# Swapping the two factors of a forward transform: 64 points first, then 47

## The chip, the cores and the metric

The kernel runs on one core of one Trainium2 chip. The metric is device time in microseconds (us) for one execution of the whole program; lower is better. Engines are named as in the profile: PE (matrix multiply) with PEld (its weight load), DVE, ACT, POOL and SP. DMAs are issued from the queues of SP, ACT and POOL.

## The reference

```python
def _attn_ref(x, w_r, w_i, b_r, b_i):          # x: (8, 3008, 256)
    X = np.fft.rfft(x, axis=1)
    Yr = X.real @ w_r - X.imag @ w_i + b_r
    Yi = X.real @ w_i + X.imag @ w_r + b_i
    Yr = np.sign(Yr) * np.maximum(np.abs(Yr) - 0.01, 0.0)
    Yi = np.sign(Yi) * np.maximum(np.abs(Yi) - 0.01, 0.0)
    return np.fft.irfft(Yr + 1j * Yi, n=3008, axis=1)

def _moe_ref(x, w_in, w_out):                   # x: (24064, 256), d_ff = 2048
    h = x @ w_in
    g = np.where(h > 0.0, h, np.exp(np.minimum(h, 0.0)) - 1.0)
    return g @ w_out
```

The output is the second function applied to the first one's result: a real Fourier transform along the sequence, a complex 256 x 256 product with a soft threshold, the transform back, and then a two-layer network with ELU over all 24064 rows.

## The kernel before

The sequence length is 3008 = 47 x 64, and each transform is done in two factor steps with matmuls against tables of sines. There are five kinds of unit work per batch, each a group of matmuls into one PSUM tile and one copy out of it:

- **A** (`unit_A`, matmul L126): the 47-point step. A chunk of x, `xts[ci]`, holds 94 rows in partitions 17 to 110 (the 17 others are zeroed in the first batch) and 8 sequence places of 256 columns. One unit is two matmuls of 512 columns; the copy (L109 or L107, 96 x 1024) goes to a tile A and from there to DRAM (DA). Eight units a batch, from four chunks.
- **X** (`unit_X`, L160): the 64-point step. `load_Z` reads DA back as Z, transposed between partitions and free dimension by that trip through DRAM: 128 partitions, 24 frequencies, 256 columns. One unit is 8 matmuls with Z as weights and 128 columns of the table M2; ACT copies 1024 columns to XT. Six units a batch, two for each group of 8 frequencies.
- **M** (`unit_M`, in the first batch `first_M`; L179): the complex product with `wcat_r` and `wcat_s`, four matmuls of 512 columns, bias on DVE (L186), soft threshold on POOL (L194, L195; in the first batch on POOL, ACT or DVE in turn). Twelve a batch. M needs the XT tile of its group of 8 frequencies.
- **B** (`unit_B`, L227): the 64-point step back with table M3; copy to Bz (L240), stored to DRAM (DB). Six a batch.
- **Y** (`unit_Y`, L267): the 47-point step back with table M4 from Bs, which `load_Bs` reads from DB: 8 matmuls of 96 rows and 94 columns and one copy of 752 columns, which gathers from PSUM with a stride. Eight a batch.

The second network works on blocks of 512 rows and pairs of 128 hidden columns: `front` (four matmuls of 512 columns, L594, then Exp on ACT), `elu`, and `back` (eight matmuls of 256 columns, L651), two slots behind. One batch is 6 blocks x 8 pairs = 48 slots. The transform units of the next batch (X, M, B), the A units of the batch after that and the Y units are fillers: `plan` puts at most one into each slot by a list written out by hand, and in a slot PE runs the filler, then `front`, then an earlier `back`. Every engine runs its own instructions in program order, and so does each queue.

```python
        mid = [
            ("X", 0), ("X", 1), ("M", 0, 0), ("M", 0, 1), ("X", 2), ("M", 1, 0), ("M", 1, 1),
            ...
            ("M", 5, 1), ("A", 0), ("B", 4), ("A", 1), ("B", 5), ("A", 2), ("A", 3), ("A", 4),
            ("A", 5), ("A", 6), ("A", 7),
        ]
```

Ahead of the slots stands the start. POOL makes index rows with iota and issues the loads of x (eight DMAs a batch, two for each chunk); DVE makes the phases and ACT the sines of M1 and M2 in three groups of 512 columns; between them the eight A units of batch 0 run with their copies and stores. Then Z is loaded, half from SP's queue and half from ACT's; M4 and M3 are made of M1 and M2 with transposes on PE. Once the second group of Z has landed (`gate`), POOL issues x of batch 1; SP issues `w_in`. X, M and B of batch 0 follow, the Bz tiles are stored (two buffers for three tiles), Bs is loaded, the eight A units of batch 1 run, w_in is scaled, and two Y units open the first slot. `idle_pe(n)` is n matmuls of 512 columns on constants, whose result is not used.

Of the kernel before, what the change touches and what calls it, by code (L numbers as in the profile page):

```python
# [12 lines left out]
F32R = mybir.dt.float32r  # L13

# [4 lines left out]
N1 = 47  # L19
# [3 lines left out]
P0 = N2 - N1  # L23
P1 = P0 + 2 * N1


@with_exitstack
def kernel(
# [23 lines left out]
    SIN_SCALE = 2.0 * math.pi / S * (1.0 - 3e-7)  # L52

    constp = ctx.enter_context(tc.tile_pool(name="constp", bufs=1))
    M1 = constp.tile([P1, 4 * K1], F32R, name="M1")
    M2 = constp.tile([P, 2, K1, N2], BF16, name="M2")
# [7 lines left out]
    lam_n = constp.tile([P, 1], F32, name="lam_n")  # L64

# [4 lines left out]
    wk4 = ctx.enter_context(tc.tile_pool(name="wk4", bufs=4))  # L70

# [23 lines left out]
    def load_x(b, ci):  # L95
        xv = x[b].rearrange("(r m c) d -> c r m d", c=4, m=8)
        for r0, r1 in ((0, 80), (80, 2 * N1)):
            nc.gpsimd.dma_start(xts[ci][P0 + r0 : P0 + r1], xv[ci, r0:r1].bitcast(F32R))

# [11 lines left out]
    def unit_A(b, u, alone=False, on_dve=False, ahead=False):  # L111
        ci, uu = u // 2, u % 2
        if uu == 0:
            if ahead and ci > 1:
                A_of[b, ci] = late3.tile([4 * K1, 8, D], BF16, name="A", tag="gT")
            elif alone:
                A_of[b, ci] = wk4.tile([4 * K1, 8, D], BF16, name="A", tag="Bs")
            else:
                A_of[b, ci] = wk2.tile([4 * K1, 8, D], BF16, name="A", tag="A")
            if ci == 0:  # L120
                DA_of[b] = dram.tile([NH, 4 * K1, D], BF16, name="DA", tag="DA")
        xt, A = xts[ci], A_of[b, ci]
        dav = DA_of[b].rearrange("(m c) r d -> c r m d", c=4)
        ps = unit_ps("aps", alone or ahead)
        for j in range(2):
            nc.tensor.matmul(  # L126
                ps[0 : 4 * K1, j, :], lhsT=M1[:],
                rhs=xt[:, 4 * uu + 2 * j : 4 * uu + 2 * j + 2, :], start=True, stop=True,
            )
        evac(  # L130
            A[:, 4 * uu : 4 * uu + 4, :].rearrange("p n d -> p (n d)"),
            ps[0 : 4 * K1].rearrange("p a b -> p (a b)"), on_dve,
        )
        if alone:
            nc.sync.dma_start(dav[ci, :, 4 * uu : 4 * uu + 4, :], A[:, 4 * uu : 4 * uu + 4, :])
        elif uu == 1:
            (nc.sync if ahead else nc.scalar).dma_start(dav[ci], A[:])

    def load_Z(b, k0, k1, n0, n1, engs):

        if b not in Z_of:
            Z_of[b] = zp.tile([P, K1, D], BF16, name="Z", tag="Z")
        for c in range(2):
            for h in range(2):
                r = h * 2 * K1 + c * K1
                q = c * N2 + h * NH
                engs[c].dma_start(
                    Z_of[b][q + n0 : q + n1, k0:k1, :], DA_of[b][n0:n1, r + k0 : r + k1, :]
                )

    def unit_X(b, u, alone=False, split=False):
        g, dt = u // 2, u % 2
        if dt == 0:
            XT_of[b, g] = wk3.tile([P, 2, 2, 8 * N2], BF16, name="XT", tag="XT")
        XT, Z = XT_of[b, g], Z_of[b]
        ps = unit_ps("xps", alone)
        psv = ps[:].rearrange("p a (k j) -> p (a k) j", j=P)
        for kk in range(8):
            k = 8 * g + kk
            nc.tensor.matmul(  # L160
                psv[:, kk, :], lhsT=Z[:, k, dt * P : dt * P + P], rhs=M2[:, :, k, :],
                start=True, stop=True,
            )
        xv = XT[:, dt].rearrange("p c (k j) -> p c k j", j=N2)
        pv = psv.rearrange("p k (c j) -> p c k j", c=2)
        if split:
            nc.scalar.copy(xv[:, :, 0:4], pv[:, :, 0:4])  # L167
            nc.vector.tensor_copy(xv[:, :, 4:8], pv[:, :, 4:8])
        else:
            nc.scalar.copy(xv, pv)  # L170
# [3 lines left out]
    def m_group(b, q, i, ps):  # L174
        XT = XT_of[b, q // 2]
        o = (2 * (q % 2) + i) * P
# [108 lines left out]
    idle_pe(20)  # L285
    xts = []
    for ci in range(4):
        xt = constp.tile([P1, 8, D], F32R, name=f"xt{ci}")
        xts.append(xt)
    with tc.tile_pool(name="stagep", bufs=1) as stagep:  # L290
# [4 lines left out]
        def iota(shape, name, pattern, base=0, cm=0):  # L295
            t = stagep.tile(shape, F32, name=name)
            nc.gpsimd.iota(
                t[:], pattern=pattern, base=base, channel_multiplier=cm,
# [4 lines left out]
        def col(name, src, s1, op0, s2=None, op1=None):  # L303
            t = stagep.tile([P, 1], F32, name=name)
            if op1 is None:
                nc.vector.tensor_scalar(t[:], src[:], s1, None, op0)
            else:
                nc.vector.tensor_scalar(t[:], src[:], s1, s2, op0, op1)
            return t

        def flat(t):
            return t.rearrange("p a b -> p (a b)")

        def zero_rows(ci):
            for m in range(0, 8, 2):
                nc.scalar.activation(
                    xts[ci][0:P0, m : m + 2, :].rearrange("p n d -> p (n d)"), busy[0:P0, :],
                    AF.Copy, scale=0.0,
                )

        pcol = iota([P, 1], "pcol", [[0, 1]], cm=1)
        k1row = iota([P1, 2, K1], "k1row", [[0, 2], [1, K1]])
        ph1 = iota([P1, 2, K1], "ph1", [[QUARTER, 2], [0, K1]], base=QUARTER)
        load_x(0, 0)
        kv = iota([P, K1, N2], "kv", [[1, K1], [N1, N2]])
        for ci in range(1, 4):
            load_x(0, ci)
        for ci in range(2, 4):
            nc.gpsimd.memset(xts[ci][0:P0].bitcast(F32), 0.0)
        ident = stagep.tile([P, P], F32, name="ident")  # L330
        nc.gpsimd.memset(ident[:], 0.0)
        nc.gpsimd.affine_select(
            out=ident[:], in_=ident[:], pattern=[[-1, P]], compare_op=ALU.not_equal,
            fill=1.0, base=0, channel_multiplier=1,
        )

        def wrap(v, r):
            nc.vector.tensor_scalar(r, v, 1.0 / S, CMAGIC, ALU.mult, ALU.add)
            nc.vector.tensor_scalar(r, r, -CMAGIC, -float(S), ALU.add, ALU.mult)
            nc.vector.tensor_tensor(v, r, v, ALU.add)  # L340


        half = col("half", pcol, 0.5, ALU.mult, -0.5 * P0 - 0.25, ALU.add)
        halfm = col("halfm", half, CMAGIC, ALU.add)
        n1col = col("n1col", halfm, -CMAGIC, ALU.add)
        n1s = col("n1s", n1col, float(N2), ALU.mult)
        v1 = stagep.tile([P1, 2 * K1], F32, name="v1")
        r1t = stagep.tile([P1, 2 * K1], F32, name="r1t")
        nc.vector.scalar_tensor_tensor(
            v1[:], flat(k1row[:]), n1s[0:P1, :], flat(ph1[:]), ALU.mult, ALU.add,  # L350
        )
        wrap(v1[:], r1t[:])
        zero_rows(0)
        nc.scalar.activation(r1t[:], v1[:], AF.Sin, bias=0.0, scale=SIN_SCALE)
        zero_rows(1)
        h1col = stagep.tile([P, 1], F32, name="h1col")
        nc.vector.scalar_tensor_tensor(
            h1col[:], n1col[:], -2.0, pcol[:], ALU.mult, ALU.add
        )
        h1col = col("h1m", h1col, float(-P0), ALU.add)  # L360
        isx = col("isx", pcol, P0 - 0.5, ALU.is_gt)
        h0col = stagep.tile([P, 1], F32, name="h0col")
        nc.vector.scalar_tensor_tensor(
            h0col[:], h1col[:], -1.0, isx[:], ALU.mult, ALU.add
        )
        nc.vector.tensor_tensor(h0col[:], h0col[:], isx[:], ALU.mult)
        nc.vector.tensor_tensor(h1col[:], h1col[:], isx[:], ALU.mult)
        ccol = col("ccol", pcol, N2 - 0.5, ALU.is_gt)
        n2col = stagep.tile([P, 1], F32, name="n2col")
        nc.vector.scalar_tensor_tensor(  # L370
            n2col[:], ccol[:], -float(N2), pcol[:], ALU.mult, ALU.add
        )
        ph2col = col("ph2col", ccol, -float(QUARTER), ALU.mult, float(QUARTER), ALU.add)
        M1f = stagep.tile([P1, 2, 2 * K1], F32, name="M1f")
        nc.vector.tensor_scalar(M1f[:, 0, :], r1t[:], h0col[0:P1, :], None, ALU.mult)
        nc.vector.tensor_scalar(M1f[:, 1, :], r1t[:], h1col[0:P1, :], None, ALU.mult)
        nc.vector.tensor_copy(M1[:], flat(M1f[:]))

        v2 = stagep.tile([P, K1, N2], F32, name="v2")
        u2 = stagep.tile([P, K1, N2], F32, name="u2")  # L380
        st = stagep.tile([P, K1, N2], F32, name="st")
        r2 = stagep.tile([P, 8, N2], F32, name="r2")

        def phases(g):

            gs = slice(8 * g, 8 * g + 8)
            nc.vector.tensor_scalar(
# [391 lines left out]
```

## Time and profile before

| what | value |
|---|---|
| three timed runs, median (lowest to highest) | 968.99 us (966.66 to 969.65) |
| the profiled execution's own time | 967.69 us |
| its span, first to last instruction | 965.8 us |
| granted PE clock, mean | 0.984 |
| PE / ACT / DVE / POOL busy | 96% / 74% / 76% / 30% |
| DMA traffic | 105.43 MB, 109 GB/s on the mean |

In the rows of a group a line reads: line, engine, operation, output <- inputs, shapes, count | busy time, mean ns of one | idle time of the engine before it and what ended that. In a window row each engine has its busy time and in brackets its count of instructions; then come the granted clock, the mean share of the 16 DMA engines (over 1 where packets overlap on one engine) and GB/s. In a timeline row and in the chain, the first number is the start in us from the first instruction and the second the duration.

### The profile page before, as it was taken

What the parts mean: (1) busy time and instruction counts of PE and PEld (TensorE: products, weight loads), DVE (VectorE), ACT (ScalarE), POOL (GpSimd) and SP (SyncE); (2) the same over time, 40 slices, a digit from 0 to 9 for tenths busy, and PEclk for the clock granted to TensorE, in tenths of its full rate; (3) what the DMA queues carried; (4) which work ended last, traced back from release to release, by engine and by line L of the source; (5) the groups of instructions that cost most, each with busy time, mean ns of one, the idle gap of its engine ahead of it and who ended that gap; (6) DMA issues with size and microseconds to landing.
All of it is one profiled execution on the core that took longest, in us unless ns stands there. A gap on an engine that the chain in (4) does not pass through costs nothing.

```text
span 965.8 us, 16747 instructions
## 1 busy us (share of the span) xinstructions
PE 927.7 (96%) x6482; PEld 654.1 (68%) x6482; DVE 737.0 (76%) x858; ACT 719.1 (74%) x816; POOL 286.5 (30%) x363
## 2 busy tenths in 40 slices
PE   7968999999999999999999999999999999999997
PEld 3425766777667766777667776677767776677775
DVE  8646677776778777886778767887778877888996
ACT  7436878688877778778786888877887788667654
POOL 5602531234302432125312343024421133321332
PEclk9959999999999999999999999999999999999999
DMA  9998824637176533827256461665338102411011
GB/s 215 239 239 182 129 77 125 165 59 129 45 191 122 87 77 82 223 52 118 67 142 159 67 125 50 181 133 87 77 82 212 32 22 67 109 45 41 23 44 42
DMA packets 113987, 105.43 MB, mean 109 GB/s; under 512 B 7794, under 2 KB 107636, under 8 KB 113012
## 3 DMA queue, kind: packets, MB, share of 16 engines
q1 hardware_dynamic: 45220, 56.19, 22.2%
q0 software_dynamic: 27680, 26.74, 19.4%
q10 hardware_dynamic: 41008, 21.43, 8.4%
q8 instruction: 51, 0.84, 0.4%
q14 instruction: 28, 0.23, 0.1%
HBM read 54.53 MB, written 49.81 MB: 108 GB/s over the span
## 4 chain that ended last, share of the span: by engine, by line
PE 59%; DVE 17%; ACT 13%; DMA 4%; issue 4%; ACTq 1%; POOL 1%; DVEq 0%; SPq 0%; POOLq 0%
PE ps_o L651 23%; PE hps L594 23%; PE mps L179 7%; DVE gT L614 6%; DVE gT L618 4%; ACT Et L604 3%; DVE Et L629 2%; PE aps L126 2%; ACT Et L601 2%; DVE Et L631 2%; ACT A L109 2%; DMA DA<-A 2%; ACT osb L663 2%; PE bps L227 1%; DMA DB<-Bz 1%
## 5 line engine op out<-in xcount | busy, mean ns | idle before, releaser
L651 PE MATMUL ps_o<-w_out_r,gT 128*128 128x256 f32 (+1 forms) x3072 | 490.5, 302 | 1.5 <-DVE gT L614 0.9
L651 PEld LDWEIGHTS ps_o<-w_out_r,gT 128*128 128x128 f32 (+1 forms) x3072 | 409.4, 187 | 66.3 <-DVE gT L614 13.0
L594 PE MATMUL hps<-yT,w_in_s 128*128 128x512 bf16 (+1 forms) x1536 | 389.0, 375 | 9.0 <-DVE gT L618 5.6
L604 ACT ACTIVATE Et<-hps 128x1024 f32<-128x1024 f32 (+1 forms) x300 | 302.2, 1007 | 104.1 <-PE hps L594 82.4
L614 DVE SCALAR_TENSOR_TENSOR gT<-Et,hps 128x1024 fp32r<-128x1024 f32 (+1 forms) x188 | 222.5, 1183 | 70.6 <-ACT Et L602 50.0
L618 DVE SCALAR_TENSOR_TENSOR gT<-hps,Et 128x1024 fp32r<-128x1024 f32 (+1 forms) x196 | 237.8, 1213 | 17.7 <-PE ps_o L651 1.5
L594 PEld LDWEIGHTS <-w_in_s 128*128 128x128 bf16 x1536 | 133.3, 98 | 150.2 <-issue 33.2
L631 DVE TENSOR_SCALAR Et<-Et 128x1024 f32<-128x1024 f32 (+1 forms) x196 | 134.6, 687 | 76.9 <-ACT Et L604 74.4
L629 POOL TENSOR_SCALAR Et<-Et 128x512 f32<-128x512 f32 (+1 forms) x104 | 64.7, 622 | 309.6 <-ACT Et L604 309.6
L194 POOL TENSOR_SCALAR clip<-yb 128x512 f32<-128x512 f32 x84 | 51.8, 616 | 293.4 <-DVE yb L186 231.2
L601 ACT ACTIVATE Et<-hps 128x1024 f32<-128x1024 f32 x84 | 86.5, 1029 | 68.6 <-PE hps L594 68.4
L195 POOL TENSOR_TENSOR Y<-yb,clip 128x512 bf16<-128x512 f32 x84 | 107.5, 1279 | 7.0
L186 DVE TENSOR_TENSOR yb<-mps,bias_bc 128x512 f32<-128x512 f32 x96 | 65.8, 689 | 34.6 <-PE mps L179 30.7
L602 ACT ACTIVATE Et<-Et 128x1024 f32<-128x1024 f32 x84 | 88.9, 1058 | 2.7
L109 ACT CAST A<-aps 96x1024 bf16<-96x1024 f32 x59 | 59.3, 1009 | 17.0 <-PE aps L126 11.0
L109 ACT CAST yT<-yps 128x752 bf16<-128x752 f32 x63 | 49.7, 790 | 14.9 <-PE yps L267 14.9
L179 PE MATMUL mps<-wcat_r,XT 128*128 128x512 bf16 x192 | 58.1, 383 | 0.3 <-ACT XT L167 0.2
L126 PE MATMUL aps<-xt,M 111*96 111x512 f32 x128 | 44.0, 436 | 14.1 <-ACT Bz L240 5.2
L629 DVE TENSOR_SCALAR Et<-Et 128x512 f32<-128x512 f32 (+1 forms) x104 | 56.8, 547 | 0.5 <-ACT Et L604 0.2
L179 PE MATMUL mps<-wcat_s,XT 128*128 128x512 bf16 x192 | 57.1, 379 | 0.0
L240 ACT CAST Bz<-bps 128x1024 bf16<-128x1024 f32 x47 | 47.4, 1008 | 9.7 <-DMA DB<-Bz 5.7
L170 ACT CAST XT<-xps 128x1024 bf16<-128x1024 f32 x46 | 46.0, 1001 | 7.9 <-PE xps L160 7.9
(96 smaller groups left out, 415.1 us busy)
## 6 DMA issues: line engine op xcount, KB each, us to landing
xt<-in_x_dram POOLq DMA_DIRECT2D x32, 640.0 KB, 6.1
out_dram<-osb SPq DMA_DIRECT2D x160, 128.0 KB
Bs<-DB SPq DMA_DIRECT2D x63, 192.0 KB
DB<-Bz ACTq DMA_DIRECT2D x21, 512.0 KB
DA<-A ACTq DMA_DIRECT2D x24, 384.0 KB
Z<-DA SPq DMA_DIRECT2D x28, 256.0 KB
Z<-DA SPq DMA_DIRECT2D x34, 128.0 KB
xt<-in_x_dram POOLq DMA_DIRECT2D x32, 112.0 KB, 5.8
```

What stands on the lines that cost most here:

```text
L109: nc.scalar.copy(dst, src)
L179: nc.tensor.matmul(ps, lhsT=XT[:, dt, c, o : o + P], rhs=wm[:, dt, :], start=(m == 0 and dt == 0), stop=(m == 1 and dt == 1),)
L195: nc.gpsimd.tensor_tensor(Y_of[b, q][:, i, :], yb[:], clip[:], ALU.subtract)
L594: nc.tensor.matmul(hps[:, s, 0:nb], lhsT=w_in_s[:, dt, ft * P : ft * P + P], rhs=yT[:, dt, bs : bs + nb], start=(dt == 0), stop=(dt == 1),)
L601: nc.scalar.activation(E_, hps[:, :, 0:nb], AF.Relu, scale=-1.0)
L602: nc.scalar.activation(E_, E_, AF.Exp, scale=-1.0)
L604: nc.scalar.activation(E_, hps[:, :, 0:nb], AF.Exp)
L614: nc.vector.scalar_tensor_tensor(gT[:, :, 0:nb], E_, -1.0, h_, ALU.add, ALU.max)
L618: nc.vector.scalar_tensor_tensor(gT[:, :, 0:nb], h_, 0.0, E_, ALU.max, ALU.add)
L629: eng.tensor_scalar(E_[:, s], E_[:, s], 1.0, 0.0, ALU.min, ALU.max)
L631: nc.vector.tensor_scalar(E_, E_, 1.0, -1.0, ALU.min, ALU.add)
L651: nc.tensor.matmul(po[q][0 : t1 - t0, i_ % 2, :], lhsT=gT[:, s, t0:t1], rhs=w_out_r[:, ft, :], start=(ft == 0 and i_ % 2 == 0), stop=(ft = ...
```

## The change

The two factors of the forward transform change places. The 64-point step comes first: x stands in 128 partitions (64 places at a 47 KB pitch in DRAM, and two halves of 24 places, which share one place), 8 places of 256 columns contiguous for each partition, so that three chunks hold a batch instead of four, and a load of a chunk is one DMA instead of two. A has six units with 128 output rows. The 47-point step follows in X: Z has 96 partitions and 32 frequencies, one unit has 8 matmuls of 96 columns, and there are eight units. The stores to DA are contiguous for 8 places (4 KB), and the loads of Z take pieces of 512 bytes. XT is one tile for the whole batch, and every M needs all eight X units; so `plan` and the start put all X ahead of all M. In the first batch the copies of X go to ACT and DVE in turn.

The tables: M1 and M2 get other phases, M2 in four groups of 384 columns from integer indices (an AND with 63 on DVE); M3 is no longer transposed from M2 but made of phases and four sines of 768 columns of its own, M4 on POOL. A first sine on a dummy loads ACT's table at the start, and the Exp table is loaded after B of batch 0. The `idle_pe` counts change: 20 to 9, 14 to 10, 10 to 6, and 2 after each of the first five A units instead of 4, 4 and 3.

The diff, cut to its core:

```diff
-    M2 = constp.tile([P, 2, K1, N2], BF16, name="M2")
+    M2 = constp.tile([2 * NR, NS, 2, 2 * K1], BF16, name="M2")      # 96 x 32 x 2 x 48
...
-    def load_x(b, ci):
-        xv = x[b].rearrange("(r m c) d -> c r m d", c=4, m=8)
-        for r0, r1 in ((0, 80), (80, 2 * N1)):
-            nc.gpsimd.dma_start(xts[ci][P0 + r0 : P0 + r1], xv[ci, r0:r1].bitcast(F32R))
+    def load_x(b, ci, m0=0, m1=8):
+        src = bass.AP(
+            tensor=x.tensor,
+            offset=x.offset + (b * S + 8 * ci + m0) * D,
+            ap=[[N1 * D, N2], [(NJ - 1) * D, 2], [D, m1 - m0], [1, D]],
+        )
+        nc.gpsimd.dma_start(xts[ci][:, m0:m1, :], src.bitcast(F32R))
...
-                ps[0 : 4 * K1, j, :], lhsT=M1[:],
+                ps[:, j, :], lhsT=M1[:],
...
     def load_Z(...):
-        for c in range(2):
-            for h in range(2):
-                r = h * 2 * K1 + c * K1
-                q = c * N2 + h * NH
-                engs[c].dma_start(
-                    Z_of[b][q + n0 : q + n1, k0:k1, :], DA_of[b][n0:n1, r + k0 : r + k1, :]
-                )
+        for c in range(2):
+            engs[c].dma_start(
+                Z_of[b][c * NR : c * NR + NR, s0:s1, :],
+                DA_of[b][c * NS + s0 : c * NS + s1].rearrange("s n d -> n s d"),
+            )
...
     def unit_X(...):
-                psv[:, kk, :], lhsT=Z[:, k, dt * P : dt * P + P], rhs=M2[:, :, k, :],
+                psv[:, kk, 0 : 4 * K1], lhsT=Z[:, k, dt * P : dt * P + P],
+                rhs=M2[:, k].rearrange("p c m -> p (c m)"), start=True, stop=True,
...
-            nc.scalar.copy(xv, pv)
+        xv = XT[:, dt].rearrange("p c (m s) -> p c m s", s=NS)[:, :, :, 8 * g : 8 * g + 8]
+        pv = psv[:, :, 0 : 4 * K1].rearrange("p k (c m) -> p c m k", c=2)
+        evac(xv, pv, on_dve)
...
+        def phases(g):                       # DVE, four groups
+            dve.tensor_scalar(m_, m_, 63, None, ALU.bitwise_and)
+            dve.scalar_tensor_tensor(k_, m_, float(N1), kk1[...], ALU.mult, ALU.add)
+            dve.tensor_scalar(v, kf, n1s[z], ph[z], ALU.mult, ALU.add)
+            dve.tensor_scalar(r, v, CMAGIC, -CMAGIC, ALU.add, ALU.add)
+            dve.tensor_tensor(v, v, r, ALU.subtract)
+            dve.tensor_scalar(st[z, gs], kf, S // 2 + 0.5, -0.5, ALU.is_gt, ALU.add)
+        def signs(g):                        # DVE; waits for sizes(g)
+            dve.scalar_tensor_tensor(a2[z, gs], a2[z, gs], qd[z], st[z, gs], ALU.subtract, ALU.mult)
+        def sizes(g):                        # ACT
+            nc.scalar.activation(a2[z, gs], v2[z, gs], AF.Abs)
...
+        sizes(3)
+        sines(2, 1)
+        signs(3)
+        slot0()
+        sines(3, 0)
+        sines(3, 1)
+        nc.scalar.activation(r4[:], v4[:], AF.Sin, bias=0.0, scale=TURN)
+        for g in range(4):
+            load_Z(0, 8 * g, 8 * g + 8, (nc.sync, nc.scalar))
...
+        nc.scalar.activation(a3[:], w3[:], AF.Abs)
+        dve.scalar_tensor_tensor(u3[:], a3[:], 0.25, st3b, ALU.subtract, ALU.mult)
...
+    for u in range(8):
+        unit_X(0, u, alone=True, on_dve=bool(u % 2))
+    for (c, o), src, sc, bi in (...):        # four sines of 128 x 768
+        nc.scalar.activation(M3[:, :, c, o * N2 : o * N2 + N2], src[:], AF.Sin, bias=bi, scale=sc)
     first_M(0, 0, nc.gpsimd)
-    fX(2)
     first_M(0, 1, nc.scalar)
...
-    for u in range(8):
+    for u in range(6):
         unit_A(1, u, on_dve=bool(u % 2), ahead=True)
...
-    idle_pe(10)
+    idle_pe(6)
...
+        mid = [("X", u) for u in range(8)] + [
+            ("M", 0, 0), ("M", 0, 1), ("M", 1, 0), ("M", 1, 1), ("B", 0), ("M", 2, 0),
+            ("M", 2, 1), ("B", 1), ("M", 3, 0), ("M", 3, 1), ("B", 2), ("M", 4, 0),
+            ("M", 4, 1), ("B", 3), ("M", 5, 0), ("M", 5, 1), ("A", 0), ("B", 4), ("A", 1),
+            ("B", 5), ("A", 2), ("A", 3), ("A", 4), ("A", 5),
+        ]
```

437 lines of the change are left out of this document (239 added, 198 removed), and 5 rows, old and new, of the table mid.

## The prediction

> **What bounds the kernel now.** I read the page first, then stages, then the chain, then single slots. The profiled execution took 967.69 us around a span of 965.8; the three timed runs have a median of 968.99, so a sum made on the profile is carried over by adding 1.3.
>
> ```profile
> PE 927.7 (96%) x6482; PEld 654.1 (68%) x6482; DVE 737.0 (76%) x858; ACT 719.1 (74%) x816; POOL 286.5 (30%) x363
> ...
> PEclk9959999999999999999999999999999999999999
> DMA  9998824637176533827256461665338102411011
> ```
>
> PE is full, except in the first three slices of 24 us, where the DMA engines are full instead and the granted clock once falls to a half. Before the first L594 matmul at 73.4 us nothing of the second network runs. From there the batches take 117.3 us, six times 113, and 99.6. The windows of that start and of one steady batch:
>
> ```profile
> 51.50:56.70 5.20, 0.03 (x1) 0.03 (x1) 0.00 (x0) 1.09 (x2) 0.00 (x0) 0.50 0.87 227
> 56.70:73.40 16.70, 13.50 (x42) 5.50 (x43) 7.86 (x9) 6.09 (x7) 2.25 (x3) 0.55 0.95 242
> ...
> 416.60:529.60 113.00, 112.29 (x806) 80.63 (x804) 86.82 (x97) 89.84 (x101) 32.80 (x40) 1.00 0.51 111
> ```
>
> The steady batch is 99% PE; the start has a 5.2 us hole and then a clock of 0.55. The chain of the first 80 us says what the start waits for:
>
> ```profile
> 21.84 1.28 ACT L447
> ...
> 25.99 5.02 DMA Z<-DA
> 31.82 5.22 POOL xt L98 x8
> ...
> 43.98 11.52 DMA DB<-Bz
> ...
> 57.86 2.27 DMA DB<-Bz
> ```
>
> To 20.5 us it is DVE making phases, then sines and a table load on ACT, which hold ACT's half of the Z loads; then eight x loads issued on POOL ahead of POOL's first soft threshold; then a store of Bz that takes 11.5 us, because x of batch 1 and w_in are on the DMA engines; then unit_A of batch 1. In the steady state the price of a filler unit is the distance of two L594 starts:
>
> ```profile
> 418.79 1.03 PE L594 MATMUL hps<-yT,w_in_s 128*128 128x512 bf16 x4
> ...
> 420.95 1.03 PE L594 MATMUL hps<-yT,w_in_s 128*128 128x512 bf16 x4
> ...
> 425.60 1.02 PE L594 MATMUL hps<-yT,w_in_s 128*128 128x512 bf16 x4
> ...
> 427.87 1.03 PE L594 MATMUL hps<-yT,w_in_s 128*128 128x512 bf16 x4
> ```
>
> A slot with a Y unit lasts 2.16, with an X unit 2.27; by the same reading A slots last 2.28 to 2.67, a bare slot 1.72 to 1.99.
>
> **The steady state.** Per batch 6 X + 8 A units become 8 X + 6 A: the same 32 fillers besides Y, so no bare slot is won or lost. A new X unit has 8 matmuls of 96 rows and 96 columns and a copy of 768 elements gathered with a stride from PSUM. That is a Y unit (96x94, 752 elements, copy 790 ns on ACT against 1001 for X today), so I price it at 2.16. A new A unit keeps two 512-column matmuls and one 1024-column copy, whose time goes by columns: same price. In the batch from 416.6, the six X slots sum to 14.37 and the eight A slots to 19.20. About 0.27 is added in the slots that follow a block's osb copies, whatever their kind (a Y slot there takes 2.49 as an X slot does), so this part stays. After: 8 X = 2.49 + 2.43 + 6 x 2.16 = 17.88; 6 A = 19.20 minus the last two (2.43, 2.38) = 14.39; the 0.27 of the X slot that becomes a B slot stays. 33.57 becomes 32.54: -1.0 a batch, for the six batches that have both kinds, -6.2; batch 6 has no A and comes out even. PE alone gives -0.85 (4 matmuls of 512 columns at 213 ns), so most does not hang on ACT. Bounds: the scattered write of the copy could cost up to 1.3 us, above any 1024-column copy here; the slot would be 2.35 and two thirds of the gain gone (-2 in all). If the ACT-bound run of A slots eases more, -9. M now stands four in a row at first; M slots take 2.69 wherever they stand, so that is nothing. load_Bs is two slots later; Bs was issued 82 us into a batch and first used near 105, so 5 us later is covered.
>
> **The start, up to M.** M1 needs the iotas, the same DVE columns and no zero_rows: 6.9 us for 6.7. DVE then makes 4 groups of 384 instead of 3 of 512. A 512-column step costs 0.34 to 0.46 (one input) or 0.70 (two); scaled, a group is 2.9 with the integer and (0.3, or 0.5 at the one-column rate), so signs end near 18.6 against 20.5. A group was held 2.3 us while POOL ran memsets; now POOL runs short columns and four wcat copies there: 0 to 3 us more. ACT runs after the last A copy: three Abs and sines more than it can finish earlier, about 9 steps of 0.5, and no Exp load (1.28, moved behind B, where ACT waits 3.8 us for DB stores anyway). x arrives as 6 pieces instead of 4 chunks; alone, its 1 KB packets moved at 200 to 220 GB/s, w_in's 2 KB ones at 330 to 350, the 8 KB ones of Z at 225. So x needs 9 to 14 us instead of 14.4 and the last A copy ends near 17.5 to 19. ACT reaches the Z loads at 23.2 (21.5 to 26) against 24.66. The 24 transposes and three copies of M3 (2.74 on PE, 2.07 on DVE) go from beside the Z transfer: nothing won.
>
> Two waits are added there. DVE's u3 waits for ACT's Abs of a3, which is queued behind ACT's four Z issues (4 x 0.43): 25.8, u3 done near 26.8, while X1's copy, queued on DVE behind it, is due at 27: covered, and 1 us if not. The four sines of M3 (768 columns, about 0.9 each by the 0.63 of 512) stand on ACT between the last X copy and the first threshold of M(0,1): ACT is free again near 37, B0 is due at 38.3; with that cover gone up to 2 us, which lie in E's bounds below. The w_r and w_i loads move from SP to the end of POOL's x issues, landing near 18, and are needed at M.
>
> Z moves the small pieces from the DA store to the load: 3072 of 512 B. No load here has 512 B pieces; 512 B stores take 27 to 31 ns, 1 KB loads of w_r on the hardware queue 46, crowded x loads of 1 KB 160 (packet records of the trace). Per engine 192 packets: 5.8 us at 30, 11.5 at 60, against 6 today. I take 35, nearest to the stores on the same queue: 6.7. The Trainium skill (DMA: Bandwidth & Descriptors, Specifications) puts line rate at 512 B and up, by which it would be an estimated 4.4 us at its 358 GB/s; no run here shows it. All eight X units must now end before the first M: last Z landing near 32, X and its copy 1.6, first M at 33.3 against 30.95.
>
> **M to B.** POOL has three x issues for eight (5.22 becomes 2.2), done before M: the 1.6 us wait of B0 and the late POOL go. From M, 5 M units at about 1 us, then the 12.4 us that B0 to B5 take today: B ends near 51, as today's 51.5. But PE has no work from the end of idle_pe (about 20) to X (26.5). In the trace a hole of 5.2 us put the clock to 0.50, and 0.55 lasted to 73.4; so the first M units run at half, 0.85 more each, three of them: +2.5, B at 53. The Trainium skill (TensorE: Matmul & The Clock Gate, Part 1: The HAM clock gate) speaks against this change in the same way: an idle window of about 3.4 us halves the clock, and the hole is longer. By it alone the loss would be an estimated 2 to 3 us; the trace agrees.
>
> The hole at 51.5 goes if the first two DB stores land earlier. x of batch 1 and w_in, 5.2 MB, start about 2 us earlier and move at 225 to 330 GB/s, so they end between 45 and 53 instead of 56. Then E, the end of the last Bz copy, is 53 to 54 against 57.1: -3.5 (-6.5 to +1).
>
> **A of batch 1 and first fronts.** Two A units fewer: u6 and u7 cost 68.16 - 65.67 = 2.5. idle_pe 10 to 6 at 0.427: -1.7, of which about 0.9 comes back as cold Y and L594 matmuls. Bs lands E + 7.5, PE reaches Y at E + 10.5: still behind. Sum -3.3 (-4.2 to -2). In batch 0 the X slot of 3.59 waits for Z: DA lands sooner as its stores start ahead of w_out, but X units 2 to 7 follow at once and need the second, larger Z load: 0 (-1.3 to +3).
>
> **Sum.** -6.2 - 3.5 - 3.3 + 0 = -13: 954.7 for the profiled execution, 956.0 beside the median.
>
> **Rivals.**
> 1. Only the steady part arrives (0.14): table chain and Z eat what the start gains. For: DVE sets the start now. 962.8.
> 2. Only the start arrives (0.08): strided copies make X slots 2.3. 962.2.
> 3. DMA decides the start fully (0.05): x at 330 GB/s, clock kept: 21 less, 948.
> 4. Slower (0.07): the 512 B pieces of Z at the price of crowded x packets, 160 ns, with w_in and x of batch 1 beside them: 192 x 0.16 = 30.7 us instead of 6.7, +24, of which the hole no longer absorbs any: 956 + 24 = 980. It turns the sign where a packet costs 0.035 + 13/192 = 0.10 us. Against: packets of this size on the hardware queues averaged 63 ns in their slowest 2 us, with x still beside them.
> 5. It does not do what it says (0.06): x still in 1 KB pieces, slow as today, and Z at 60 ns: start +6, steady -6: 969, no change.
>
> **Numbers.** My forecast has 0.60. What the runs can tell from no change is 0.3%, 2.9 us. Faster: 0.60 + 0.14 + 0.08 + 0.05, less 0.02 for tails of rival 1: 0.85; same 0.07; slower 0.08. The low end takes the gains' bounds (-6.5, -4.2, -9, -1.3: 948), the high end the losses' (+1, -2, -2, +3 and a little: 969), of which I cut 2: 947 to 967.
>
> **What would show it.** Right: L594 distances of about 2.16 in X slots; six batches of 112; first L594 near 66; no gap of 5 us on PE before A of batch 1; Z packets under 45 ns; clock below 1 at the first M. Wrong: X slots at 2.3; Z landing after 36; the first L594 after 71.

## The result and the profile after

The changed kernel takes 955.88 us (median of four runs, 955.64 to 956.73) against 968.87 for the kernel before on the same chip (four runs, 966.66 to 969.65). The ratio is 0.9871, with a 95% interval of 0.9854 to 0.9888. The profiled execution took 955.73 us around a span of 953.9, where before it was 967.69 around 965.8.

The page of the changed kernel; the lines are busy time of each engine, and two lines of the 40 slices:

```profile
PE 909.9 (95%) x6430; PEld 649.0 (68%) x6533; DVE 737.5 (77%) x867; ACT 712.3 (75%) x819; POOL 272.4 (29%) x364
...
PEclk8689999999999999999999999999999999999999
DMA  8979225813176213932249231671228201321011
```

PE lost 18 us of busy time and the span 12; a part of the 18 is records that the trace lacks (6430 matmuls beside 6533 weight loads, where before there were 6482 of each). The clock is reduced in the first three slices (0.8, 0.6, 0.8), where before it was the third alone (0.5). The DMA engines, 0.8 to 0.9 busy in the first five slices before, are at 0.2 in the fifth now. The windows of the changed kernel show it stage by stage (length, busy time of PE, PEld, DVE, ACT and POOL, granted clock, DMA share, GB/s):

```profile
30.00:36.40 6.40, 4.80 (x48) 3.76 (x47) 3.25 (x4) 4.16 (x6) 1.55 (x3) 0.50 1.01 351
36.40:54.00 17.60, 15.81 (x95) 6.62 (x95) 13.43 (x20) 10.65 (x14) 10.73 (x10) 0.93 0.65 227
54.00:65.20 11.20, 7.32 (x32) 3.68 (x33) 6.65 (x8) 6.23 (x8) 2.23 (x3) 0.70 0.77 201
407.60:519.90 112.30, 110.76 (x803) 80.14 (x814) 86.69 (x97) 88.98 (x101) 29.18 (x35) 1.00 0.43 112
```

The hole of 5.2 us before A of batch 1 is gone. The clock is halved earlier instead, while X and the first M run; from the last Bz copy to the first front it is 0.70 and not 0.55, and that stretch takes 11.2 us instead of 16.3. A steady batch takes 112.3 instead of 113. The chain of the first 80 us, changed kernel:

```profile
20.54 0.41 POOL v L488
...
21.55 0.67 POOL v L490
...
22.48 5.37 DMA Z<-DA
...
36.38 3.48 PE mps L185 x10
...
54.81 0.76 DMA DB<-Bz
...
57.86 1.02 ACT A L119
```

The store of Bz, 11.5 us on the chain before, is 0.76 now. In the place of the table load on ACT stand POOL's short columns for M4, which the prediction had only as a possible delay of DVE. And the X slots of the steady state, by starts of the front matmuls (L674, once L594):

```profile
420.94 1.03 PE L674 MATMUL hps<-yT,w_in_s 128*128 128x512 bf16 x3
423.11 1.03 PE L674 MATMUL hps<-yT,w_in_s 128*128 128x512 bf16 x4
425.28 1.03 PE L674 MATMUL hps<-yT,w_in_s 128*128 128x512 bf16 x4
427.44 1.03 PE L674 MATMUL hps<-yT,w_in_s 128*128 128x512 bf16 x3
```

They are 2.17 apart, 0.10 less than before. That is PE's part: a unit's first matmul starts 0.35 us ahead of its front, where before it was 0.45 (427.42 to 427.87). The strided copy, which might have undone it, takes 809 ns for 768 elements, against 1001 for 1024 before.

```profile
L119 ACT CAST XT<-xps 128x768 bf16<-128x768 f32 x60 | 48.5, 809 | 18.3 <-PE xps L170 18.3
```

**Where the 11.9 us of the span went.** A batch is taken from the first weight load of its first front. Batch 1 begins at 183.0 instead of 190.7 us: -7.7, made up of -8.2 at the first front (65.22 for 73.42 by its matmuls) and about +0.4 in batch 0 (118.5 for 118.1). Batches 1 to 5 take 561.6 instead of 565.0 (-3.4), batch 6 110.3 instead of 110.5 (-0.2), the rest 99.05 instead of 99.65 (-0.6).

### The profile page after: what moved, and what is told of

It reads as the page before. It is cut to its first block, busy times and chain, and to the rows that moved or that the text cites. A ratio compares the mean times of both kernels' runs of the same rounds, so it can differ in the third digit from the quotient of the medians.

```text
span 953.9 us, 16669 instructions
## 1 busy us (share of the span) xinstructions
PE 909.9 (95%) x6430; PEld 649.0 (68%) x6533; DVE 737.5 (77%) x867; ACT 712.3 (75%) x819; POOL 272.4 (29%) x364
## 4 chain that ended last, share of the span: by engine, by line
PE 48%; DVE 22%; ACT 16%; issue 6%; DMA 3%; POOL 2%; ACTq 1%; DVEq 0%; SPq 0%; POOLq 0%
PE hps L674 19%; PE ps_o L731 18%; DVE gT L694 10%; DVE gT L698 5%; ACT Et L684 5%; PE mps L185 4%; DVE Et L709 4%; ACT Et L681 3%; ACT Bz L246 2%; ACT osb L743 2%; PE xps L170 2%; DVE Et L711 2%; DMA Z<-DA 2%; PE aps L136 2%; ACT A L119 2%
## 5 line engine op out<-in xcount | busy, mean ns | idle before, releaser
L731 PEld LDWEIGHTS ps_o<-w_out_r,gT 128*128 128x128 f32 (+1 forms) x3072 | 411.0, 187 | 69.3 <-DVE gT L694 11.9
L674 PE MATMUL hps<-yT,w_in_s 128*128 128x512 bf16 (+1 forms) x1462 | 383.5, 375 | 11.2 <-DVE gT L698 3.7
L694 DVE SCALAR_TENSOR_TENSOR gT<-Et,hps 128x1024 fp32r<-128x1024 f32 (+1 forms) x186 | 220.0, 1183 | 62.6 <-ACT Et L682 45.0
L698 DVE SCALAR_TENSOR_TENSOR gT<-hps,Et 128x1024 fp32r<-128x1024 f32 (+1 forms) x198 | 240.3, 1214 | 19.7 <-PE ps_o L731 2.5
L674 PEld LDWEIGHTS <-w_in_s 128*128 128x128 bf16 x1536 | 131.6, 98 | 145.5 <-issue 29.7
L709 POOL TENSOR_SCALAR Et<-Et 128x512 f32<-128x512 f32 (+1 forms) x102 | 62.7, 614 | 280.3 <-ACT Et L684 280.3
L119 ACT CAST XT<-xps 128x768 bf16<-128x768 f32 x60 | 48.5, 809 | 18.3 <-PE xps L170 18.3
L709 DVE TENSOR_SCALAR Et<-Et 128x512 f32<-128x512 f32 (+1 forms) x102 | 56.2, 551 | 0.4 <-ACT Et L684 0.4
L119 ACT CAST A<-aps 128x1024 bf16<-128x1024 f32 x45 | 45.5, 1013 | 12.4 <-PE aps L136 10.1
L185 PE MATMUL mps<-wcat_r,XT 128*128 128x512 bf16 x172 | 54.3, 388 | 0.2 <-DVE yb L192 0.2
L185 PEld LDWEIGHTS <-XT 128*128 128x128 bf16 x384 | 31.0, 99 | 30.9 <-issue 2.9
L743 ACT COPY osb<-ps_o 128x512 f32<-128x512 f32 x88 | 47.3, 588 | 2.9 <-PE ps_o L731 2.9
```

The source lines that it names most:

```text
L119: nc.scalar.copy(dst, src)
L185: nc.tensor.matmul(ps, lhsT=XT[:, dt, c, o : o + P], rhs=wm[:, dt, :], start=(m == 0 and dt == 0), stop=(m == 1 and dt == 1),)
L674: nc.tensor.matmul(hps[:, s, 0:nb], lhsT=w_in_s[:, dt, ft * P : ft * P + P], rhs=yT[:, dt, bs : bs + nb], start=(dt == 0), stop=(dt == 1),)
L694: nc.vector.scalar_tensor_tensor(gT[:, :, 0:nb], E_, -1.0, h_, ALU.add, ALU.max)
L698: nc.vector.scalar_tensor_tensor(gT[:, :, 0:nb], h_, 0.0, E_, ALU.max, ALU.add)
L709: eng.tensor_scalar(E_[:, s], E_[:, s], 1.0, 0.0, ALU.min, ALU.max)
```

## The experiments

Each kernel is the changed one with the edit shown; one edits the kernel before, and is marked so. Each ratio is to the kernel before on the same chip; the medians come from several chips, on which that kernel took 967.1 to 968.9. Slots are counted from 0 in their batch, those of batch 0 by weight loads, those of steady batches by starts of front matmuls (the expectations count the latter by weight loads too, which moves some by one). One yardstick is needed for the start: the two kernels with other Y slots, untouched up to the first fronts (their slots are worth some 0.5 us in batch 0), begin batch 1 at 182.3 and 183.2 us, the changed kernel at 183.0. So a profile tells the start to about 1 us.

**What holds ACT's half of Z** (5 rounds). The sine of r4 waits for POOL's columns, and ACT's four Z issues are queued behind it.

```diff
-        nc.scalar.activation(r4[:], v4[:], AF.Sin, bias=0.0, scale=TURN)
         for g in range(4):
             load_Z(0, 8 * g, 8 * g + 8, (nc.sync, nc.scalar))
+        nc.scalar.activation(r4[:], v4[:], AF.Sin, bias=0.0, scale=TURN)
```

> The changed kernel with one line moved: the sine of r4 stands behind ACT's four Z issues instead of ahead of them. In the changed kernel's timeline that sine waits until 22.24 us for POOL's phases of M4, and ACT's half of Z is issued behind it at 22.48, though ACT was done with the tables at 20.5. Theory A (the wait for POOL holds the start): ACT issues Z near 20.5, the two halves move side by side, the last Z lands 1.5 to 2 us earlier, the first M and the first L674 matmul follow: 954 to 954.5 us for 955.9. Rival B (the pieces of 512 bytes keep the DMA engines at some 145 GB/s whichever half is asked for): Z lands less than 0.5 us earlier, 955.5 to 956.

953.13 us (952.60 to 953.74), ratio 0.9840 (0.9822 to 0.9859). The timeline of the changed kernel, with what ended the idle time in brackets, and then that of this kernel:

```profile
22.24 0.24 ACT L527 ACTIVATE r<-v 128x47 f32<-128x47 f32 x1 [1.77 <-POOL v L490]
22.48 1.92 ACTq L156 DMA_DIRECT2D Z<-DA  x4
```

```profile
20.02 1.88 SPq L156 DMA_DIRECT2D Z<-DA  x4
20.12 1.92 ACTq L156 DMA_DIRECT2D Z<-DA  x4
...
24.23 1.33 PE L170 MATMUL xps<-M,Z 96*128 96x96 bf16 x16 [3.29 <-DMA Z<-DA]
```

ACT issues 2.4 us earlier and the first X starts at 24.23 instead of 27.95. Of these 3.7 us the steady run of M keeps 3.0 (33.4 for 36.38), the first back matmul, which waits for w_out (below), 2.2 (70.73 for 72.90), and batch 1 begins at 181.0, 1.3 to 2.2 ahead of the yardstick and the changed kernel. The medians differ by 2.7 us, more than the 1.4 to 1.9 that was expected. The intervals of the two ratios just touch, but the whole chain of starts moved: POOL's columns did hold ACT's half of Z, and cost 2 to 3 us.

**Whether small pieces slow Z** (3 rounds). Each partition reads runs of 4 KB, not eight pieces of 512 B.

```diff
-                DA_of[b][c * NS + s0 : c * NS + s1].rearrange("s n d -> n s d"),
+                DA_of[b][c * NS + s0 : c * NS + s1].rearrange("s n d -> (s n) d")
+                .rearrange("(n s) d -> n s d", s=s1 - s0),
```

> The changed kernel with the loads of Z reading the same bytes in runs of 4 KB (12 KB in the second load of later batches) instead of pieces of 512 bytes, so the places of Z stand in another order and the transform's values are not the reference's; everything else is the same work. Theory A (the small pieces cost): Z of batch 0 moves in about 6 us instead of 9.1 (20.8 to 29.9 us), the last X and the first M come 2.5 to 3 us earlier, about 953 us. Rival B (the ports of 48 partitions set the rate): no earlier than 1 us, 955 to 956. Steady batches stay at 112.3 in both.

954.38 us (952.71 to 954.86), ratio 0.9850 (0.9830 to 0.9870). The first X starts at 27.84 instead of 27.95, the gate on POOL, which waits for the second of Z's four groups, comes at 28.72 instead of 29.14, and the last packet of Z ends at 28.86 instead of 29.46. With the larger runs 193 to 205 GB/s were moved between 22 and 26 us against 135 to 138 (ACT's half joined in at 23.7 us, against 25.0), but the transfer ends with the half that ACT issues late. So at the start the pieces of 512 B cost 0.1 to 0.6 us, and the late half the rest. The median is 1.5 us lower, but batch 1 begins at 181.6, 0.7 ahead of the nearer yardstick, and the intervals of the ratios overlap: whether the pieces cost anything further on is not settled.

**Whether idle_pe and the A units still set the first front** (5 rounds).

```diff
-    idle_pe(6)
+    idle_pe(10)
```

> The changed kernel with ten matmuls without use ahead of the first Y unit, as before the change, instead of six. Theory A (they stand on the path at the full clock, which the changed kernel shows there: five in 1.24 us): four more at 0.216 are 0.9 us, 956.7 to 956.9. Rival B (at half the clock, as I had predicted): 1.7 us, 957.6. Rival C (Bs is later than PE there): nothing, 955.9.

955.82 us (955.48 to 956.64), ratio 0.9868 (0.9849 to 0.9886): no difference. In the profile the first front moves from 65.22 to 68.81, and batch 0 gives back 2.2 us of the 3.6 (116.3 for 118.5; its slot 3 takes 3.22 instead of 6.75). So something behind the first front sets most of that stretch's end. In the timeline of the changed kernel it has a name:

```profile
62.77 1.24 PE L289 MATMUL ips<-busy 128*128 128x512 bf16 x5
...
72.90 2.08 PE L731 MATMUL ps_o<-w_out_r,gT 128*128 128x256 f32 x8 [2.19 <-DMA w_out_r<-in_moe_w_out_dram]
```

The first back matmul waits for w_out, whose load is held by the gate on Bs.

**w_out earlier** (5 rounds). Its first half goes behind x of batch 1.

```diff
         load_x(1, ci)
+    load_w_out(0)
 ...
     gate(Bs_of[0, 0][:, 0, 0:1])
-    load_w_out(0)
     load_w_out(1)
```

> The changed kernel with the load of the first half of w_out issued on POOL right behind x of batch 1 instead of behind the landing of Bs. Theory A (the first fronts no longer wait for A or Bs but the first back waits for w_out: slot 3 of batch 0 takes 6.75 us, and with ten idle matmuls the first L674 came 3.6 us later at no cost): slot 3 goes back to about 3.2, 952 to 953 us. Rival B (w_out then holds the stores of Bz, as x did before the change, and B ends later by what the first back wins): 955 to 957.

952.77 us (952.04 to 954.10), ratio 0.9845 (0.9823 to 0.9867). In its timeline the back matmuls follow the third front at once:

```profile
70.89 1.02 PE L674 MATMUL hps<-yT,w_in_s 128*128 128x512 bf16 x4 [0.89 <-DVE gT L698]
71.57 1.29 PE L731 MATMUL ps_o<-w_out_r,gT 128*128 128x256 f32 x8
```

Slot 3 takes 3.20 instead of 6.75 and batch 0 113.9 instead of 118.5, while the first front is 1.2 later; batch 1 begins at 179.6, 2.7 to 3.6 ahead of the yardstick. The medians differ by 3.1, and the intervals of the ratios overlap by a little; the trace decides. The wait for w_out is shown to be the bound that took the place of the wait for Z in batch 0.

**Both together, and ACT's Bs issue on SP** (5 rounds).

```diff
-        load_Bs(0, w, (nc.sync, nc.sync if w else nc.scalar))
+        load_Bs(0, w, (nc.sync, nc.sync))
```

> The changed kernel with three moves together: the sine of r4 behind ACT's Z issues (alone 953.1), the first half of w_out behind x of batch 1 (alone 952.8), and the one Bs issue of ACT's queue given to SP, so that ACT need not wait for the stores of DB before its first copy of A of batch 1. Theory A (they lie one behind the other on the start's chain): first L674 near 62, batch 0 near 114, 949 to 950.5 us. Rival B (what is won before Bs is lost in waiting for w_out's second half or for Z of batch 1): 952 to 953.

952.29 us (950.29 to 952.78), ratio 0.9842 (0.9824 to 0.9860). It is the lowest median here, but not to be told from either part alone: 2.7 and 3.1 do not add, as rival B had it. In the profiled execution, the fastest of the five at 950.29, the first front comes at 63.02 and batch 1 begins at 178.0, but batch 0 takes 114.9. Its slot 7 lasts 4.10, and the chain shows the next wait, A of batch 1 through DA to Z:

```profile
61.07 7.64 DMA DA<-A
70.26 9.54 DMA Z<-DA
```

**Where a short slot should stand** (5 rounds each). First Y units 6 and 7 before the X units, then in slots 19 and 27, where osb copies fall.

```diff
-            lead, seq = int(b == 0), [("y", u) for u in range(2, 6)] + mid
-            seq.insert(20, ("y", 6))
-            seq.insert(24, ("y", 7))
+            lead, seq = int(b == 0), [("y", u) for u in range(2, 8)] + mid
```

> The changed kernel with Y units 6 and 7 in slots 4 and 5, ahead of all X, instead of between the M and B units (slots 20 and 24). Theory A: the steady batch gained 0.7 us instead of the predicted 1.0 because an M slot that follows a Y slot in that run stalls (3.12 us in slot 22 and 3.21 in slot 29, where PE waits for gT, against 2.52 to 2.69 for the other M slots), so without a Y among them both stalls go: 0.9 us a batch, 7 batches, 949.5 to 950.5 us. Rival B: the stall is owed to the osb copies of each block and only moves to another M or B slot: 955 to 956.5.

```diff
-            seq.insert(20, ("y", 6))
-            seq.insert(24, ("y", 7))
+            seq.insert(19, ("y", 6))
+            seq.insert(27, ("y", 7))
```

> The changed kernel with Y units 6 and 7 in slots 19 and 27 (those that follow a block's osb copies on ACT), so that B0 to B3 move by a slot. Theory A (new, after the run with Y in slots 4 and 5 came out slower at 113.0 a batch): ACT is behind by the two osb copies in slots 3, 11, 19, 27 and 35 of a batch; an X or a Y slot, with 1.8 us of ACT work in 2.17, takes that up, a B slot (2.03 and later) hands it on, and the second M slot behind pays 0.4 to 0.5. With Y in both slots the M slots of 3.1 and 3.2 go to 2.7: 0.7 to 1.0 a batch, 949 to 951 us. Rival B (M slots pay wherever the osb copies are): a batch stays at 112.3, 955 to 957.

958.95 us (958.60 to 959.57), ratio 0.9901 (0.9885 to 0.9917), and 958.41 us (957.02 to 959.13), ratio 0.9901 (0.9881 to 0.9921): both slower than the changed kernel, with steady batches of 113.0 and 112.65. In the first, an M slot of 3.5 appears and the M sum rises to 33.7 a batch from 33.0. In the second, Y in slot 19 takes 2.44 and in slot 27 2.99, and M in slot 28 3.28. Neither theory had either result. A Y unit does not take up an osb copy better than a B unit, whose slots with one take 2.73 instead of 2.45: its own take 0.27 more, or 0.8.

**What the osb copies cost** (3 rounds each). In both kernels only 8 of the 256 columns are copied and stored; for the kernel before the same lines are edited.

```diff
-                nc.scalar.copy(osb[:, 2 * q : 2 * q + k, :], po[q][:, 0:k, :])
+                nc.scalar.copy(osb[:, 2 * q : 2 * q + k, 0:8], po[q][:, 0:k, 0:8])
 ...
-                        ov[w, r0 : r0 + n8], osb[p0 : p0 + 8 * n8, i_, :]
+                        ov[w, r0 : r0 + n8, :, 0:8], osb[p0 : p0 + 8 * n8, i_, 0:8]
```

> The changed kernel with osb copies and output stores of 8 of the 256 columns (the rest of the output is left out). In pair with the kernel before, changed alike. Theory A (the shortfall of the steady gain, 0.7 for 1.0 us a batch, comes from where the osb copies fall): without them the stalls of slots 19, 22, 27, 29 and 35 go, a batch is near 110 us and 1.0 us or more below the kernel before with the same cut. Rival B (the shortfall has nothing to do with them): the distance between the two stays 0.6 to 0.7 us a batch.

> The kernel before with osb copies and output stores of 8 of the 256 columns (the rest of the output is left out). Theory A: a steady batch near 111.2, that is 1.0 us or more above the changed kernel with the same cut. Rival B: 0.6 to 0.7 above it.

945.44 us (944.00 to 945.63) for the changed kernel, ratio 0.9766 (0.9748 to 0.9785); 960.11 us (958.89 to 962.06) for the kernel before, ratio 0.9923 (0.9901 to 0.9944). Batches 1 to 5 together take 554.2 and 560.3, which is 110.8 and 112.1 a batch where 110 and 111.2 were expected. So the full copies cost 4.7 us over these five batches before the change (565.0 less 560.3) and 7.4 after it (561.6 less 554.2): 0.9 and 1.5 a batch. Without them the change is worth 6.1 us over five batches, 1.23 each. That mean hides two levels: the kernel before with short copies takes 112.4 and 112.5 in batches 1 and 2, where slots without a filler are longer, and 111.8 in the other three, in which the change is worth 0.93 (and 0.72 with full copies). So the osb copies account for 0.2 to 0.5 of a batch. Slot by slot, full against short, a copy adds 0.23 to 0.31 where it falls on X, Y or B and nothing where it falls on M: before on X in slots 4, 11 and 19, and for free on M in 27; after on X in 4 and on B in 19 and 27, and for free on M in 12 (with Y moved up, slot 12 holds an X, and it takes 2.46). The A slots, which carry the rest, lose 0.60 a batch instead of 0.34. What does not go away, against theory A, is a wait in M: 3.12 before (slot 26), 3.10 and 2.98 after (slots 21 and 29), where with full copies it is 3.13, and 3.13 and 3.00. The timeline of the changed kernel and that of the same kernel with short copies both have it:

```profile
458.40 1.02 PE L674 MATMUL hps<-yT,w_in_s 128*128 128x512 bf16 x4 [0.28 <-DVE gT L698]
```

```profile
452.75 1.02 PE L674 MATMUL hps<-yT,w_in_s 128*128 128x512 bf16 x4 [0.25 <-DVE gT L698]
```

**What made x slow before** (3 rounds each). While batch 1's x, by the traces the load that kept the DB store waiting, was on its way, 198 to 233 GB/s were moved before and about 415 now, with w_in beside it. The change altered the size of the pieces, the addresses and the partitions together. Two kernels go back to 1 KB pieces in 128 partitions, 23 KB and 20 KB apart; the third goes back to the old shape for batches 1 and up, 94 rows in 80 and 14 partitions from partition 17.

```diff
-            offset=x.offset + (b * S + 8 * ci + m0) * D,
-            ap=[[N1 * D, N2], [(NJ - 1) * D, 2], [D, m1 - m0], [1, D]],
+            offset=x.offset + (b * S + ci + 4 * m0) * D,
+            ap=[[23 * D, P], [4 * D, m1 - m0], [1, D]],
```

> The changed kernel with x read in pieces of 1 KB at a 4 KB step, partitions 23 KB apart, the same number of bytes but other rows, so its values are not the reference's. Theory A (large pieces are what ends the two x bursts earlier): x of batch 0 and of batch 1 move near 210 GB/s as before the change instead of 330 to 400, x of batch 1 ends near 50 instead of 43.5 us, the stores of Bz wait for it and the hole ahead of A comes back: 959 to 962 us. Rival B (the pieces do not matter, the tables and POOL hold the first burst and nothing waits for the second): 955.5 to 957.

The second differs from it by 20 in the place of 23.

> As the run with 1 KB pieces of x, but partitions 20 KB apart, so that all pieces of one chunk lie in the same quarter of each 4 KB of DRAM, as they did before the change; other rows again, and values that are not the reference's. Theory A (it is the size of the pieces that slowed x before): the same as partitions 23 KB apart, within 0.5 us and 5% of the rate. Rival B (it is their common place in each 4 KB): packets of 150 to 165 ns here against 60 to 110 there, and 2 to 4 us more.

```diff
+        if b > 0:
+            xv = x[b].rearrange("(r m c) d -> c r m d", c=4, m=8)
+            for r0, r1 in ((0, 80), (80, 2 * N1)):
+                nc.gpsimd.dma_start(xts[ci][17 + r0 : 17 + r1], xv[ci, r0:r1].bitcast(F32R))
+            return
```

> The changed kernel with x of all batches but the first loaded as before the change: 94 rows in partitions 17 to 110, two DMAs of 80 and 14 partitions for a chunk, 1 KB pieces at a 4 KB step (three chunks, so a quarter of the bytes is not read, and values are not the reference's). The 128-partition loads in 1 KB pieces moved at 340 to 350 GB/s in this kernel. Theory A (the shape of the DMA, 80 rows beside 14 from partition 17 on, held x to 210 GB/s before the change): the packets of x of batch 1 take 150 to 180 ns again and 190 to 220 GB/s are moved; with 2.3 MB it ends near 47 to 49 us instead of 43.5, and the total is 956 to 958. Rival B (it was what ran beside it, not the shape): 80 to 95 ns and 330 GB/s or more, 955 to 956.

956.51 us (955.35 to 957.51), ratio 0.9882 (0.9858 to 0.9907); 956.62 us (955.65 to 957.06), 0.9881 (0.9852 to 0.9909); 956.23 us (955.23 to 957.60), 0.9882 (0.9862 to 0.9902). None is told from the changed kernel. In the profiles of the two with 1 KB pieces for all batches, batch 1 begins at 185.1 and 184.7, 1.5 or more behind the changed kernel and both yardsticks, so a cost of the smaller pieces in batch 0's x is not excluded. And the rates differ: the windows of the changed kernel, of 1 KB pieces 23 KB apart, and of the old shape, all from 42 or 38 us on:

```profile
38.00:42.00 4.00, 4.00 (x23) 1.69 (x21) 2.97 (x6) 0.83 (x2) 3.07 (x4) 0.91 1.07 415
```

```profile
42.00:46.00 4.00, 4.00 (x28) 1.71 (x28) 3.75 (x7) 1.98 (x3) 3.34 (x4) 1.00 1.90 349
```

```profile
38.00:42.00 4.00, 4.00 (x22) 1.71 (x22) 3.08 (x6) 0.72 (x1) 2.88 (x4) 0.90 2.02 215
42.00:46.00 4.00, 4.00 (x29) 1.71 (x26) 3.50 (x5) 3.17 (x4) 3.74 (x4) 1.00 2.02 202
```

From 42 to 46 us, with x alone on the DMA engines, a 1 KB piece takes 89 ns in 128 partitions, with either step of the addresses, and 159 in the old shape. So the old shape, not the small piece, held x at about 200 GB/s; what in that shape (its 94 partitions, their start at 17, or the split into 80 and 14) was not tried. It costs no time here: the slow x ends at 49.1 us, and the first Bz store, issued at 43.72, has its first packet at 45.96. Before the change x went on to 56.2, and that store, issued at 42.42, had its first packet at 48.59. None of the three runs brought the hole of 5.2 us back, so that slow x made it is read from the traces and not shown by a run.

## Why the prediction was right, and where its terms were not

**The total.** 956.0 stood against 955.88. The sum was -13 on the profiled execution, which moved by 12.0 (967.69 to 955.73). The rest is that the kernel before had been profiled 1.3 below its median and the changed one 0.2 below its own. So that the medians meet within 0.2 us is luck; the gain was 1.0 too large. Within the sum, the terms up to the start of batch 1 (-3.5, -3.3, 0, and -1.0 for batch 0's share of the steady gain) make -7.8, and -7.7 was measured; batches 1 to 5 gave 3.4 of the other 5.2, and batch 6 and the rest 0.8, for which the sum had nothing. (Of the "six times 113" it started from, the sixth is batch 6, at 110.5.)

**The steady state, -5.2 predicted for batches 1 to 5, -3.4 measured.** The price of the X unit held: 2.17 a slot for 2.16, and the feared strided copy at 1.3 us was 0.81. By starts of front matmuls over batches 1 to 5, eight X and six A take 32.25 a batch, where 17.88 + 14.39 = 32.27 was worked out, but this agreement is luck. X took 17.60, since the second osb copy falls on an M slot, where it costs nothing. A took 14.65: the sum had left out the last two A slots (2.43 and 2.38), but what went are cheaper ones, and behind the osb copy of slot 35 the slots still take 2.87, 2.41 and 2.42. The step that failed is the one on what else fills the slots. M, which "is nothing", rose by 0.28 (32.76 to 33.04), since a second M slot waits. B rose by 0.40 (14.87 to 15.27) where 0.27 was left for it: two B slots now carry an osb copy and none did (+0.56), and one that took 2.63 takes 2.45. With -1.31 for X and A and -0.06 for the bare slots that is -0.69 a batch instead of -1.0. The runs with short copies show that the osb copies have a part in this, of 0.2 to 0.5 a batch. That PE waits in the second M slot for the gT of DVE is in the trace; why there and not elsewhere was not settled, and both reorderings of Y ended slower.

**Up to M.** The table signs (19.7 us for 18.6 to 21.6) and the last A copy (16.97 for 17.5 to 19) came about as worked out. ACT reached its Z loads at 22.48 against 23.2, but not for the reason given: ACT's own sines were done at 20.47, and POOL's columns of 0.2 to 0.7 us each held r4. Where the prediction said that POOL's columns would hold DVE for 0 to 3 us, they held ACT for 1.8, and this was worth 2.7 in all. Z took 52 ns for a packet of 512 B on the mean, not 35, and 8.8 us from its first packet to its last, not 6.7 (its 8 KB pieces before, of which the prediction speaks, were of 4 KB). Even so its last packet ended at 29.5, not near 32, and X began at 27.95. The step that failed here is that X ends 1.6 after Z: eight X units in turn took 0.84 each at half clock, and X's last copy ended at 35.9. The first M was at 34.7, its steady run at 36.4, against 33.3.

**M to B.** The granted clock was 0.50 from 21.6 to 38.7 us, with a hole of 8.7 us on PE (19.24 to 27.95). The Trainium skill (TensorE: Matmul & The Clock Gate, Part 1: The HAM clock gate) has the clock halved after an idle window of about 3.4 us; the trace agrees in part, as the hole is longer, but the clock's record falls 2.4 us into it. That a hole put the old clock to 0.50 does not come out of the trace either: it fell at 51.39, and the hole began at 51.48. In the changed kernel it falls a second time, at 55.76, where PE's longest pause is 1.3 us:

```profile
52.30:55.76 3.46, 1.86 (x10) 0.71 (x7) 2.13 (x4) 2.52 (x4) 0.00 (x0) 1.00 0.54 154
55.76:59.20 3.44, 1.49 (x3) 0.77 (x4) 1.68 (x2) 1.34 (x2) 0.00 (x0) 0.50 0.54 153
```

PE was busy for 1.86 of the 3.46 us before that fall, and for 1.49 of the 3.40 before the old one. So a PE that is busy half of the time lost its clock here; at which share it falls is open. The half clock was booked on three M units (+2.5), but the X units paid most of it: M began 3.1 late, and from there to the end of B it took 17.1 us instead of 19.7. So that B ended at 53.4 for 53 is in part two errors that cancel. E, by ACT's half of the last Bz copy, was at 54.06: -3.05 where -3.5 was said. Batch 1's x ended at 44.8 us, just ahead of the 45 to 53 given, and the DB store was free, as the prediction had it.

**A of batch 1 and the first fronts, -3.3 predicted, -5.15 in this profile.** From E to the first front 16.3 us became 11.16. Up to idle_pe 2.1 of this were won, for the 2.5 of the two A units in the sum. The other 3.05 lie in idle_pe: 1.7 for four matmuls fewer, as worked out, and 1.3 for the clock, as the six that are left (the trace has five) took 1.24 us here, where 10 took 4.29 before. In three profiles of kernels with the same PE code up to there (the two with other Y slots, and w_out earlier) the five took 2.34, at half clock, the first front came at 66.4 to 66.9, and the stretch from E took 12.7. By these the term is -3.6, near the -3.3 worked out; the profile of the changed kernel had the clock back early. That is worth little, as the next wait takes it back.

**Batch 0, 0 predicted beside its share of the steady gain, +0.4 measured with that share.** The X slot's wait for Z went (3.57 to 2.17), which the sum had not counted on, and a wait for w_out came in slot 3 (3.21 to 6.75), for which the prediction did not look. The question "what is late next" was not asked of the first back matmul: w_out's gate stands behind Bs, and an earlier first front meets it. Start and batch 0 together gave 7.7 us, and 7.5 and 8.4 by the yardstick, against 7.8 predicted: the start won more than its terms, and batch 0 gave it back.

**The rivals.** The slower one needed 0.10 us for a 512 B packet beside crowded transfers. The slowest two microseconds had 0.080, and no w_in or x was moving then: they were issued at 27.99 and 29.66. "Only the start arrives" is the nearest in size, with 7.7 of 11.9 us from the start and batch 0, but its reason, slow strided copies, did not hold.

## What to carry to other kernels

Where one engine is full and units fill its slots, a unit's price is not enough: look up which slots carry the other recurring work (here the copies of results, 0.27 each), and count again which kinds of unit those slots hold after the change. A start that becomes shorter meets the next gate: list every load that is issued behind a semaphore of the start, and give each its landing time, before a gain there is booked. And ask of every short operation on a slow side engine who waits for the last of the series: thirty of them on POOL, one behind the other, took 13 us here.

## What the runs showed of the hardware that was not expected

- The shape of a load in partitions decided its rate more than the size of its pieces: 1 KB pieces into 128 partitions moved at about 349 GB/s, the same pieces into 80 + 14 partitions from partition 17 at 202 to 215, and 8 KB pieces into 128 partitions, with w_in beside them, at 413 to 415.
- Half of Z (48 partitions, from one queue, in pieces of 512 B) did not move at one rate. Alone it moved 247 GB/s from 20.8 to 22.0 us and 248 from 27 to 29, but 135 to 138 from 22 to 26, with 73 to 77 ns a packet. In the run with r4's sine moved, both halves side by side from two queues moved 262 and 224 over that same stretch. What made it slow there was not tried; POOL was busy with copies of `wcat` all through it.

```profile
22.00:24.00 2.00, 0.00 (x0) 0.00 (x0) 1.90 (x4) 0.24 (x1) 2.00 (x3) 0.50 1.26 138
27.00:29.00 2.00, 1.05 (x14) 1.08 (x15) 0.00 (x0) 0.22 (x1) 0.97 (x3) 0.50 1.22 248
```

- One-column operations on POOL (128x1) took 0.19 to 0.71 us, half of them 0.45 or more, beside a busy DVE.
- The clock came back at different points of the same code: the five idle matmuls before the first front took 1.24 us in one profile, 2.34 in three with the same PE code up to there, and 1.71 where r4's sine was moved. In the trace's record of the granted clock the half-clock stretch that begins in A of batch 1 lasts 6.83 us in the first and 10.24 in the others; all stretches of that record in these traces are whole multiples of 3.41 us.
